# An attention and expert-layer kernel: one more PSUM bank for transposes, router steps in another order, part of v from another queue

## The chip, the core and the metric

The kernel runs on one core of a Trainium2 chip. The metric is the device time of one execution in microseconds (us). The engines are TensorE (PE: matmuls and transposes, with PEld for its weight loads), VectorE (DVE), ScalarE (ACT), GpSimd (POOL) and SyncE (SP). They run side by side and wait for each other through semaphores. Transfers from and to DRAM are issued by SP or GpSimd and carried out by 16 DMA engines. Matmul results land in PSUM, eight banks of 128 x 512 numbers, and from there ScalarE or VectorE copies them to SBUF.

## The reference

There are 8 batches, 8 heads, 576 positions of width 64. Attention works within chunks of 64 positions; its result is read as 4608 tokens of width 512. Each token goes to one of 16 experts (4 groups of 4).

```python
scores = scale * np.matmul(q_c, k_c.transpose(0, 1, 2, 4, 3))        # per chunk of 64
attn = np.exp(scores - scores.max(-1, keepdims=True))
attn = attn / (attn.sum(-1, keepdims=True) + 1e-09)
x = (attn @ v_c) ...                                                 # 4608 x 512
g_idx = np.argmax(x @ w_group, axis=1)                               # softmax weight g_w
for g in range(4):
    xg = x[g_idx == g]
    e_idx = np.argmax(xg @ w_expert[g], axis=1)                      # softmax weight e_w
    for e in range(4):
        h = np.maximum(xg[e_idx == e] @ w1[g, e], 0.0)               # 512 -> 1024
        out[tokens of g, e] = (g_w * e_w)[:, None] * (h @ w2[g, e])  # 1024 -> 512
```

## The kernel before

**Stages.** Up to about 200 us a loop walks over 36 token tiles of 128 tokens (two chunks). Until about 245 us a hand-written tail finishes attention and routing and begins the first expert. Then a loop over units runs the experts: a unit is up to 256 tokens of one expert, and GpSimd gathers its rows from the DRAM buffer `xs` and scatters its results to the output.

**A step of the token loop.** The order on TensorE, ScalarE and VectorE is the order of the source; SP's and GpSimd's streams are ordered by the scheduler. Step t is a row of short names (function `run`): `b` scores of tile t (L312), `s` maximum and subtraction on VectorE (m L320, pr L324), `p` attention times v of tile t-2 (L349), `n` its normalisation into x (L365), two `a` (transposes of q and k for later tiles, L293, copied out at L297), `c` transposes of the exponentials of tile t-1 (L337, copied at L339), `e` the exponential (L331), `x` transposes of x of tile t-3 (L377, copied at L378).

**The router.** Every four tiles, `1` multiplies the transposed x with the router weights (L384) and ScalarE copies the logits to `lts` (L386); `2` transposes them back (L394 to L397); `3` ranks the tokens by matmuls (L485, L486). Between these, VectorE works through `route` and `place`, generators of which the helper `more` runs a step at a time between its other instructions; Ls, mx, one, ls (L410 to L420) come first, then ScalarE's exponential `ex` (L426). At the end GpSimd scatters the tiles' rows to `xs` (L512).

**PSUM banks.** The transposes `a`, `c` and `x` take turns with three banks (pool `pst`, tile `tp`). The router's three products share one bank, `lgk`, through the helper `bank`; the tail gives them a bank of the pool instead. Scores and outputs have two banks each.

**Loads.** q and k come in 512-KB pieces (L256) and v per head and batch: 64 partitions x 9 chunks x 256 bytes (L274), into two buffers used by turns. All of them are issued by SP, in one queue. GpSimd issues the scatters of x, and the weights and rows of the first expert (L183, L187, L562).

**Experts.** Token numbers and gate weights of a unit stand in the last two columns of its gathered rows. GpSimd copies them to `in_`, and once the scatter of the unit before has landed, from `in_` to `io_`, which VectorE multiplies with (L1045, L1049) and the scatter takes its row numbers from (L1308).

## Time and profile before

| | us |
|---|---|
| three runs | 700.09, 707.25, 702.55 (median 702.55) |
| profiled execution | 695.77, its span 694.1 |
| TensorE busy | 613.5 (88% of the span) |
| VectorE busy | 396.6 (57%) |
| ScalarE busy | 325.5 (47%) |
| GpSimd busy | 154.9 (22%) |

The profile covers one execution. A row of its timeline gives start, duration, engine, line of the kernel, operation and tiles, and in brackets how long the engine had been idle and what ended that. The view of waits sums such idle times by the instruction that waited and the one that released it. PEclk is the granted TensorE clock as a share of full speed. The DMA column is the mean busy share of the 16 DMA engines; it can pass 1 where transfers of two queues overlap on an engine.

### The profile page before, as it was taken

The numbers are of one execution on the slowest core, as the hardware profiler recorded it, in microseconds if no ns is written. First come the engines' busy times: TensorE is split into PE (matmuls) and PEld (weight loads), VectorE is DVE, ScalarE is ACT, GpSimd is POOL, SyncE is SP. The second block draws the span as 40 slices with busy tenths as digits, with TensorE's granted clock in tenths as the row PEclk, the third lists the DMA queues.
The fourth block names the chain that finished last, engine by engine and source line by source line (L and its number), as shares of the span: only waits on it lengthen the run. The fifth ranks groups of instructions, "written<-read, shape, count | busy, mean of one in ns | idle before, by whom it ended". The sixth has DMA issues, their size and how long they took to land.

```text
span 694.1 us, 16755 instructions
## 1 busy us (share of the span) xinstructions
PE 613.5 (88%) x5866; PEld 537.3 (77%) x5867; DVE 396.6 (57%) x731; ACT 325.5 (47%) x450; POOL 154.9 (22%) x256
## 2 busy tenths in 40 slices
PE   5678777777698889999899999999999999999991
PEld 4567666656576778998888889898998998898980
DVE  2557777877657657721267875572622777853220
ACT  2567777876744244611237555151611574551110
POOL 0000222223533322122123331222212212322110
PEclk9988999997879989999999999999999999999996
DMA  9989999999831298841074985644341667831000
GB/s 188 219 168 249 247 185 228 219 265 224 252 123 62 92 343 306 288 138 62 26 289 152 332 310 185 222 171 170 155 155 60 236 233 255 324 121 56 30 30 15
DMA packets 116852, 128.13 MB, mean 185 GB/s; under 512 B 49406, under 2 KB 84478, under 8 KB 116800
## 3 DMA queue, kind: packets, MB, share of 16 engines
q1 hardware_dynamic: 105936, 93.76, 48.2%
q0 software_dynamic: 10864, 33.64, 14.3%
q8 instruction: 37, 0.61, 0.4%
q14 instruction: 15, 0.12, 0.1%
HBM read 106.23 MB, written 21.93 MB: 185 GB/s over the span
## 4 chain that ended last, share of the span: by engine, by line
PE 72%; DMA 6%; DVE 6%; ACT 5%; SPq 5%; issue 3%; DVEq 0%; POOL 0%; ACTq 0%; POOLq 0%
PE py L844 26%; PE ph L829 18%; PE lgk L829 6%; PE ph L813 5%; DMA va<-in_v_dram 5%; SPq L256 2%; ACT qT L297 2%; PE tp L293 2%; PE tp L377 2%; PE py L861 2%; PE pxt L729 2%; SPq L274 1%; PE o L349 1%; PE sc L312 1%; PE ph L775 1%
## 5 line engine op out<-in xcount | busy, mean ns | idle before, releaser
L829 PE MATMUL ph<-xt,w1h 128*128 128x256 f32 x672 | 102.1, 289 | 5.4 <-issue 5.4
L829 PEld LDWEIGHTS ph<-xt,w1h 128*128 128x128 f32 x672 | 92.4, 198 | 7.2 <-issue 6.2
L984 ACT ACTIVATE hth<-ph 128x512 fp32r<-128x512 f32 x43 | 25.7, 598 | 153.3 <-PE ph L829 151.0
L1308 POOL DMA_INDIRECT out_dram<-xl,io__3479 x37 | 39.1, 1056 | 157.1 <-DVE xl L1045 141.5
L1059 DVE TENSOR_TENSOR w2l<-w2r,w2h 128x1024 fp32r<-128x1024 f32 x60 | 69.5, 1221 | 7.5 <-ACT w2h L999 5.3
L1055 DVE TENSOR_TENSOR w1l<-w1r,w1h 128x2048 fp32r<-128x2048 f32 x28 | 63.2, 2292 | 13.7 <-ACT w1h L971 11.9
L844 PE MATMUL py<-w2h,hth 128*128 128x512 f32 x264 | 67.7, 398 | 0.0
L844 PE MATMUL py<-w2l,hth 128*128 128x512 f32 x264 | 65.3, 389 | 0.0
L844 PE MATMUL py<-w2h,htl 128*128 128x512 f32 x264 | 65.2, 389 | 0.0
L1045 DVE TENSOR_SCALAR xl<-py,io__3479 128x512 f32<-128x512 f32 x33 | 24.7, 750 | 67.7 <-PE py L844 67.3
L1078 DVE SCALAR_TENSOR_TENSOR htl<-ph,hth 128x512 fp32r<-128x512 f32 x40 | 27.4, 688 | 60.3 <-ACT hth L984 59.7
L844 PEld LDWEIGHTS py<-w2l,hth 128*128 128x128 f32 x264 | 49.6, 188 | 10.6
L844 PEld LDWEIGHTS py<-w2h,htl 128*128 128x128 f32 x264 | 49.6, 188 | 10.3
L829 PE MATMUL ph<-xt,w1l 128*128 128x256 f32 x336 | 55.5, 288 | 0.5 <-DVE w1l L1055 0.5
L293 PE MATMUL tp<-cs,qk 128*128 128x128 f32 x272 | 49.0, 311 | 7.6 <-DMA qk<-in_q_dram 5.8
L844 PEld LDWEIGHTS py<-w2h,hth 128*128 128x128 f32 x264 | 47.6, 188 | 10.2 <-ACT hth L1030 0.9
L971 ACT CAST w1h<-w1r 128x2048 fp32r<-128x2048 f32 x28 | 52.2, 1903 | 4.5 <-DMA w1r<-in_moe_w_dram 2.7
L297 ACT COPY qT<-tp 64x512 f32<-64x512 f32 x68 | 41.9, 616 | 23.6 <-PE tp L293 22.9
L975 ACT CAST w2h<-w2r 128x2048 fp32r<-128x2048 f32 x28 | 52.3, 1924 | 0.0
L512 POOL DMA_INDIRECT xs<-x,pos x24 | 23.7, 986 | 119.2 <-DMA va<-in_v_dram 69.9
L829 PEld LDWEIGHTS ph<-xt,w1l 128*128 128x128 f32 x336 | 47.7, 197 | 0.7 <-DVE w1l L1055 0.7
L293 PEld LDWEIGHTS tp<-cs,qk 128*128 128x128 f32 x272 | 35.1, 159 | 16.9 <-issue 13.2
(269 smaller groups left out, 1067.9 us busy)
## 6 DMA issues: line engine op xcount, KB each, us to landing
w1r<-in_moe_w_dram SPq DMA_DIRECT2D x30, 1024.0 KB, 6.2
w2r<-in_moe_w_dram SPq DMA_DIRECT2D x30, 1024.0 KB, 6.8
xgr<-xs POOLq DMA_DIRECT2D x38, 257.0 KB, 5.4
va<-in_v_dram SPq DMA_DIRECT2D x56, 144.0 KB, 6.4
qk<-in_q_dram SPq DMA_DIRECT2D x11, 512.0 KB, 6.1
qk<-in_k_dram SPq DMA_DIRECT2D x11, 512.0 KB, 7.1
w1r<-in_moe_w_dram POOLq DMA_DIRECT2D x2, 1024.0 KB, 10.0
w2r<-in_moe_w_dram POOLq DMA_DIRECT2D x2, 1024.0 KB, 7.6
```

The costliest lines, as they stand in the source:

```text
L293: nc.tensor.transpose(pt[:, hp, :], st["q", n // 4][:, z, 2 * hp + x], ident)
L297: (nc.vector.tensor_copy if z and not a else nc.scalar.copy)(to[:, a], pt[64 * a:64 * a + 64])
L813: m = pe.matmul(ph[n], a_[:, c, 0:P], w_[:, c, n * 512:(n + 1) * 512], start=(i == 0), stop=(i == 11))
L829: m = pe.matmul(ph[f // 2][:, f % 2 * 256:f % 2 * 256 + 256], w_[:, c, f * P:(f + 1) * P], a_[:, c, :], start=(i == 0), stop=(i == 11))
L844: m = pe.matmul(py[j], a_[:, f, half[j]], w_(b, f), start=(i == 0), stop=(i == 23))
L971: lambda b, s, j: ac.copy(wt[b][0][:, s], w1r[j]), K1)
L975: lambda b, s, j: ac.copy(wt[b][2 + j], w2r[j]), K2)
L984: ac.activation(hth()[:, 2 * b:2 * b + 2, :], ph[b].rearrange("p (f t) -> p f t", f=2), AF.Relu).then_inc(S["Ha"], 1)
L1055: lambda b, s, j: ve.tensor_sub(wt[b][1][:, s], w1r[j], wt[b][0][:, s].bitcast(F32)), K1, js)
L1059: m = ve.tensor_sub(wt[b][4 + 2 * j + i], w2r[j][:, 2 * i:2 * i + 2], wt[b][2 + j][:, 2 * i:2 * i + 2].bitcast(F32))
L1078: ve.scalar_tensor_tensor(out=htl()[:, 2 * b:2 * b + 2, :], in0=ph[b].rearrange("p (f t) -> p f t", f=2), scalar=0.0, in1=hth()[:, 2 * b:2 ...
L1308: gp.indirect_dma_start(out, bass.IndirectOffsetOnAxis(ap=io[:, j, 0:1].bitcast(I32), axis=0), yb[:, j, :], None, bounds_check=N - 1, oob_ ...
```

## The change

- `bank` now deals out four banks by turns in the token loop: every fourth request, of transposes and router products alike, gets `lgk`. In the tail (`turn[0] = -1`) it deals out the pool's three, and `lgk` is used where it was before.
- The `lts` copy is a step of its own (`l`) and stands behind the first `a`; in the tail `l7` and `l8` stand one and two names further on than the copies did. `3` moves to the end of its step. The first part of each router generator, which reads a bank, runs at once behind the maximum `m` of the next step (`read_banks`). `ex` is issued two router steps later.
- v of batches 1 to 4 is loaded by GpSimd.
- Unit numbers go to two buffers by turns; `in_` and the second copy are gone, and the unit's code on GpSimd and VectorE stands twice, chosen by the unit's number.

```diff
+                (nc.gpsimd if 0 < b < 5 else nc.sync).dma_start(vbufs[b % NV][64 * x:64 * x + 64, j:, hp, 0:HD],
                                   v[b, h, j * CH:, :].rearrange("(c s) d -> s c d", s=CH))
 
             def stage_a(n):
...
                     st["T", u, i] = kpool.tile([P, 4, 512], F32, name="kT" if i else "qT", tag="qkT")
                 dst = st["T", u, i % 2]
-                pt = ps_t.tile([P, 4, P], F32, name="tp")
+                pt = heads4(bank())
...
 
-            def bank(end):
-
-                return ps_t.tile([P, 4, P], F32, name="tp").rearrange("p a b -> p (a b)") if end else lgk
+
+            turn = [0]
+
+            def bank():
+                turn[0] += turn[0] >= 0
+                if turn[0] > 0 and turn[0] % 4 == 3:
+                    return lgk
+                return ps_t.tile([P, 4, P], F32, name="tp").rearrange("p a b -> p (a b)")
+
+            heads4 = lambda z: z.rearrange("p (a b) -> p a b", a=4)
...
@@ -318,6 +325,7 @@
                 sc = s["sc"]
                 m = rpool.tile([P, 2, 4], F32, name="m")
                 nc.vector.tensor_reduce(out=m, in_=sc, axis=AX.X, op=ALU.max)
+                read_banks()
                 more()
 
...
             def stage_e1(g):
                 xT = st["xT", g]
-                lt = bank(g >= GL - 1)
+                lt = bank()
                 for c in range(4):
                     nc.tensor.matmul(lt[32 * c:32 * c + 32, :], lhsT=wg[:, c, :], rhs=xT[:, c, :], start=True, stop=True)
+                st["lt", g] = lt
+
+            def stage_lts(g):
                 lts = xtpool.tile([P, 512], F32, name="lts")
-                nc.scalar.copy(lts, lt)
+                nc.scalar.copy(lts, st["lt", g])
                 st["lts", g] = lts
 
             def stage_e2(g):
                 lts = st["lts", g]
-                lg = lgk
+                lg = lgk if turn[0] < 0 else bank()
                 for i in range(NG):
...
                 st["lg", g] = lg
-                routing.append(route(g))
+                (first if turn[0] >= 0 else routing).append(route(g))
...
                 ex = rpool.tile([P, R5, 4], F32, name="ex")
-                nc.scalar.activation(ex, ls, AF.Exp)
+                if fast:
+                    nc.scalar.activation(ex, ls, AF.Exp)
                 yield
                 V.tensor_reduce(out=mx, in_=one, axis=AX.X, op=ALU.min)
                 yield
+                if not fast:
+                    nc.scalar.activation(ex, ls, AF.Exp)
                 V.tensor_tensor(out=one, in0=one, in1=mb, op=ALU.is_equal)
...
-                rk = bank(g >= GL - 2)
+                rk = bank()
...
-                    routing.append(take(cn, n))
-                routing.append(place(g))
+                    (first if turn[0] >= 0 else routing).append(take(cn, n))
+                (first if turn[0] >= 0 else routing).append(place(g))
                 if g == GC:
-                    routing.append(choose(cn))
+                    (first if turn[0] >= 0 else routing).append(choose(cn))
...
-            routing = []
+            routing, first = [], []
+
+            def read_banks():
+                while first:
+                    z = first.pop(0)
+                    if z.gi_code.co_name != "choose":
+                        next(z)
+                    routing.append(z)
...
                     if last(t - 4):
                         run("1%d" % ((t - 4) // NG))
                     run("a%d" % (2 * t + 6) if t else FIRST)
-                    if last(t - 7):
-                        run("3%d" % ((t - 7) // NG))
+                    if last(t - 4):
+                        run("l%d" % ((t - 4) // NG))
...
                     run(" ".join("V%d" % n for n in VS.get(t, ())))
                     if last(t - 4):
                         run("2%d" % ((t - 4) // NG))
+                    if last(t - 7):
+                        run("3%d" % ((t - 7) // NG))
                     run(EXTRA.get(t, ""))
+                turn[0] = -1
                 run(TAIL)
...
-        io_, in_ = (fpool.tile([P, 2, 2], F32, name=n) for n in ("io_", "in_"))
+
+        io_ = [fpool.tile([P, 2, 2], F32, name="io%d" % i) for i in range(2)]
...
+        def by_turns(eng, u, f):
+            with eng.If((u & 1) == 0):
+                f(io_[0], io_[1])
+            with eng.Else():
+                f(io_[1], io_[0])
...
+                    def YE(j, io):
+                        return ve.tensor_scalar(out=yb[:, j, :], in0=py[j], scalar1=io[:, j, 1:2], scalar2=None, op0=ALU.mult)
+
+                    def YEh(u, j, n, io):
+                        g, y = io[0:64, j, 1:2], yb[0:64, j, :]
...
+                        def out_(io, _):
+                            def free():
                                 W("Is", 2 * u)
                                 W("Sc", 32 * u)
-                                W("L2", 2 * u + 2)
-                                YEh(u, 0, 2)
+
+                            with ve.If(k > 1):
+                                free()
+                                W("L2", 2 * u + 1)
+                                YE(0, io).then_inc(S["Y"], 1)
...
+                        by_turns(ve, u, out_)
...
-                        W("Is", 2 * u)
-                        W("XT", 2 * u + 4)
-                        carry2(in_, xg[:, :, D:XW], "In")
-                        W("In", 2 * u)
-                        gather(ra[0], 0)
-
-                        with gp.If(ra[1] < mr):
-                            gather(ra[1], 1)
+                        def unit(io, nxt):
+                            W("XT", 2 * u + 4)
+                            W("Sc", 32 * u)
+                            carry2(nxt, xg[:, :, D:XW], "Is")
+                            W("Is", 2 * u + 2)
+                            gather(ra[0], 0)
+
+                            with gp.If(ra[1] < mr):
+                                gather(ra[1], 1)
+                            with gp.Else():
+                                gp.dma_start(xg[0:1, 1, 0:1], xs[mr:mr + 1, 0:1]).then_inc(S["Gb"], 16)
+                            scatter(2 * u + 2, 0, io)
+                            with gp.If(k > 1):
+                                scatter(2 * u + 2, 1, io)
+                            with gp.Else():
+                                gp.dma_start(word, xs[mr:mr + 1, 0:1]).then_inc(S["Sc"], 16)
+
+                        by_turns(gp, u, unit)
```

ScalarE's stream at the second router step of the loop, with the copies and exponentials of two token steps; before:

```order
L386 COPY lts<-lgk 128x512
L297 COPY qT<-tp 64x4x128 x2
L339 COPY pT<-tp 128x512
L331 ACTIVATE pr<-pr 128x512
L297 COPY kT<-tp 64x4x128
L378 COPY xT<-tp 128x4x128
L426 ACTIVATE ex<-ls 128x80
L297 COPY qT<-tp 64x4x128 x2
```

and with the change:

```order
L297 COPY qT<-lgk 64x4x128 x2
L397 COPY lts<-tp 128x512
L347 COPY pT<-tp 128x512
L339 ACTIVATE pr<-pr 128x512
L297 COPY kT<-tp 64x4x128
L386 COPY xT<-tp 128x4x128
L443 ACTIVATE ex<-ls 128x80
L297 COPY qT<-tp 64x4x128 x2
```

The lts copy has moved behind the two copies of qT; ex has kept its place, and some copies now read the bank `lgk`.

VectorE's stream at the head of the step that follows, where the router's numbers are first read; before:

```order
L320 TENSOR_REDUCE m<-sc 128x8
L410 TENSOR_REDUCE Ls<-lgk 128x80
L414 TENSOR_REDUCE mx<-Ls 128x20
L324 TENSOR_TENSOR pr<-sc,m 128x2x4x64
L418 TENSOR_TENSOR one<-Ls,mx 128x80
L420 TENSOR_TENSOR ls<-Ls,mx 128x80
L424 SCALAR_TENSOR_TENSOR one<-one,cs 128x80
```

and with the change:

```order
L327 TENSOR_REDUCE m<-sc 128x8
L421 TENSOR_REDUCE Ls<-tp 128x80
L425 TENSOR_REDUCE mx<-Ls 128x20
L429 TENSOR_TENSOR one<-Ls,mx 128x80
L431 TENSOR_TENSOR ls<-Ls,mx 128x80
L332 TENSOR_TENSOR pr<-sc,m 128x2x4x64
L435 SCALAR_TENSOR_TENSOR one<-one,cs 128x80
```

The two steps that end in ls now stand ahead of the subtraction pr.

GpSimd's stream from its first fills on (`va_131` and `va_129` are the two buffers of v, `xs` the scatter's target); before:

```order
L115 MEMSET pad 128x1
L603 CAST identr<-cs 128x128
L363 CAST x<-cs 128x4 x2
L363 CAST xl<-cs 128x4
L512 DMA xs<-x,pos 75904x514 x4
L363 CAST x<-cs 128x4
L512 DMA xs<-x,pos 75904x514 x4
```

and with the change:

```order
L371 CAST x<-cs 128x4
L371 CAST xl<-cs 128x4
L274 DMA va_129<-in_v_dram 64x9x64 x8
L274 DMA va_131<-in_v_dram 64x9x64 x4
L526 DMA xs<-x,pos 75904x514 x4
L274 DMA va_131<-in_v_dram 64x9x64 x4
L371 CAST x<-cs 128x4
L274 DMA va_129<-in_v_dram 64x9x64 x2
L526 DMA xs<-x,pos 75904x514 x4
L274 DMA va_129<-in_v_dram 64x9x64 x4
```

The 32 loads now stand among the scatters; the eight of batch 1 (`va_131`) come ahead of the rows shown, among the first fills.

## Rows read from the trace of the kernel before

**Rows 1.** Busy time of each engine in three stretches; the last columns as headed.

```profile
core 0: us, PE busy (x) PEld busy (x) DVE busy (x) ACT busy (x) POOL busy (x), PEclk, DMA share, GB/s
...
26.00:164.00 138.00, 107.37 (x2293) 87.44 (x2292) 100.41 (x299) 102.60 (x178) 21.90 (x26) 0.95 1.05 226
164.00:200.00 36.00, 26.94 (x410) 22.71 (x411) 23.70 (x60) 22.43 (x40) 19.86 (x21) 0.69 0.82 214
...
245.00:694.00 449.00, 427.83 (x2659) 384.44 (x2657) 235.80 (x258) 174.96 (x192) 96.75 (x181) 0.97 0.51 179
```

**Rows 2.** The same view, first and last of four groups of four token tiles.

```profile
58.00:77.80 19.80, 15.96 (x333) 13.09 (x332) 15.00 (x45) 14.67 (x27) 3.04 (x3) 0.91 1.09 247
...
116.30:135.40 19.10, 15.54 (x337) 12.31 (x336) 15.85 (x59) 15.14 (x28) 3.36 (x5) 1.00 1.08 226
```

**Rows 3.** Waits of ScalarE, 26 to 164 us: total us, times, longest.

```profile
ACT qT L297 <- PE tp L293: 12.3, 8, 5.9
ACT ex L426 <- DVE ls L420: 10.2, 6, 2.1
ACT lts L386 <- PE lgk L384: 8.7, 6, 1.9
```

**Rows 4.** Waits of TensorE in the same stretch.

```profile
PE tp L377 <- ACT qT L297: 16.4, 23, 2.1
PE o L349 <- DMA va<-in_v_dram: 8.7, 7, 3.7
```

**Rows 5.** Timeline of TensorE: start, duration, engine, line; idle time before it in brackets.

```profile
38.79 0.69 PE L312 MATMUL sc<-kT,qT 64*64 64x64 f32 x32
...
42.46 0.69 PE L312 MATMUL sc<-kT,qT 64*64 64x64 f32 x32
...
48.13 0.94 PE L349 MATMUL o<-va,pT 64*64 64x65 f32 x6 [3.66 <-DMA va<-in_v_dram]
...
52.61 0.70 PE L312 MATMUL sc<-kT,qT 64*64 64x64 f32 x15
```

**Rows 6.** Busy time and granted clock (PEclk) behind the stall.

```profile
48.00:54.00 6.00, 5.87 (x86) 5.22 (x86) 1.95 (x5) 3.55 (x6) 0.00 (x0) 0.54 1.07 258
```

**Rows 7.** Timeline of all engines around one router step.

```profile
94.97 0.59 ACT L386 COPY lts<-lgk 128x512 f32<-128x512 f32 x1 [1.19 <-PE lgk L384]
...
95.52 1.24 ACT L297 COPY qT<-tp 64x512 f32<-64x512 f32 x2
...
97.31 0.60 PE L397 MATMUL lgk<-cs,lts 128*128 128x128 f32 x4
...
99.98 0.68 DVE L324 TENSOR_TENSOR pr<-sc,m 128x512 f32<-128x512 f32 x1
...
100.57 0.23 DVE L418 TENSOR_TENSOR one<-Ls,mx 128x80 f32<-128x80 f32 x1
...
100.99 0.27 ACT L426 ACTIVATE ex<-ls 128x80 f32<-128x80 f32 x1 [1.81 <-DVE ls L420]
```

**Rows 8.** Issue of v on SP: ns least, median, most; first and last start.

```profile
L274 SPq DMA_DIRECT2D va<-in_v_dram x64: 595/976/4343, 12.7 to 170.2; - x64
```

**Rows 9.** Timeline of GpSimd: a weight load and a scatter that it issues.

```profile
170.82 0.78 POOL L187 DMA_DIRECT2D w2r<-in_moe_w_dram  x1
...
183.62 0.96 POOL L512 DMA_INDIRECT xs<-xl,pos  x1 [0.30 <-issue]
```

**Rows 10.** DMA packets from 4 to 8, 24 to 28 and 42 to 150 us.

```profile
DMA packets 3709, 0.93 MB, mean 233 GB/s; under 512 B 3709, under 2 KB 3709, under 8 KB 3709
...
DMA packets 2249, 1.13 MB, mean 283 GB/s; under 512 B 41, under 2 KB 2249, under 8 KB 2249
...
DMA packets 49475, 23.99 MB, mean 222 GB/s; under 512 B 24972, under 2 KB 47484, under 8 KB 49456
```

**Rows 11.** Waits of TensorE and VectorE, 245 to 694 us: total us, times, longest.

```profile
PE ph L829 <- issue: 5.4, 2, 3.5
...
DVE xl L1045 <- POOL io__3479 L1303: 0.4, 1, 0.4
```

## The prediction

> **What bounds the kernel now.** I read the stages first. After 245 us TensorE is busy 427.8 of 449 us, VectorE half of it and ScalarE less [rows 1]: the expert stage is TensorE's. Before 164 us no engine is full over the stretch: TensorE 107, VectorE 100, ScalarE 103 of 138 us, with the DMA engines' share at 1.05. A group of four token tiles there takes 19.8 us at the start and 19.1 us later, while ScalarE is busy 14.7 to 15.1 us of it and VectorE 15.0 to 15.9 [rows 2]. So 4 us per group are waits, and the list of waits says whose. On ScalarE, six waits of 8.7 us together stand before the copy of the router's logits (lts), six of 10.2 us before the router's exponential (ex), and 12.3 us before copies of transposed q, which are TensorE being late [rows 3]. TensorE is late for two reasons: 16.4 us for a PSUM bank that ScalarE has not emptied, and 8.7 us for v from DRAM [rows 4]. [...]

> **ScalarE's router steps and the fourth bank.** These go together, because neither pays alone. Per group, ScalarE loses 8.7/6 = 1.45 us at lts and 10.2/6 = 1.70 us at ex. The lts copy now stands behind the two q copies (1.24 us). TensorE's router matmuls are done by then, so I take that wait as gone. The ex instruction keeps its place between xT and qT on ScalarE, though the source issues it later: what moves is its input. On VectorE ls now comes before the subtraction pr, and pr took 0.59 us from its start to the next (99.98 to 100.57) [rows 7]. What remains: from the second router step on TensorE (97.31) to ex (100.99) were 3.68 us [rows 7]; without pr 3.1, with a hand-over of some 0.2 ahead of it 3.3 us after lts ends. ScalarE's own work between lts and ex was 3.62 us (from 95.56 to 99.18, where its wait of 1.81 begins) and loses the q copies, so 2.4 us. So 0.9 us of waiting stays, and I add 0.25 because kT on ScalarE follows kT on VectorE, which does the router steps of that tile first. Gain per group: 1.45 + 1.70 - 0.9 - 0.25 = 2.0 us. Without the fourth bank TensorE would not get ahead: its 16.4 us of bank waits put it in step with ScalarE, and lts would push the next transposes back. The extra bank removes these waits, but in plain steps it wins nothing itself, as ScalarE is busy nearly all of them. The router step runs seven times in the loop; five lie in the stretch that ScalarE and VectorE hold. The last two lie where v and the first weights arrive, and count 1 us together. Sum: -11 us. Bounds: 0, if another engine holds the pace, and 7 x 3.15 = -22 us.

> **v of batches 1 to 4 on GpSimd.** Taken off SP's queue are 32 loads at a median of 0.98 us [rows 8], 31 us of issue in which q and k stood behind v. What waited for these four batches on TensorE is 3.66 us and then 2.3 of the 8.7 us; the rest belongs to batch 5, which stays on SP. With the slow clock the first stall cost 10.15 - 3.67 = 6.5 us. Gain at most 6.5 + 2.3 = 8.8 us; I take 7. GpSimd issued no load of 256-byte runs before, so its price is bounded: a weight load of 512 runs took it 0.78 us, an indirect scatter of 128 rows 0.96 us [rows 9]; a v load has 64 x 9 = 576 runs, so 0.8 us or 4.5 x 0.96 = 4.3 us. The weight load is the same kind of instruction, so I take 0.8 us. The loads of batches 3 and 4 also stand between the scatters of x in that queue, 4 x 1.3 us each time; the step that needs them is five tiles (18 us) after the buffer is free. Scatters behind a load that waits for its buffer cost nothing until the first expert is chosen.

> Against it: batch 1 is now issued in the first 10 us, beside the q and k that everything waits for. Its 8 x 576 packets are 4608/927 = 5.0 us of the DMA engines at the highest rate seen (3709 packets in 4 us) [rows 10]. Some of it falls where SP's own issue is the limit; I charge +2 us, with ends 0 and +5.

> [...]

> **Do the DMA engines allow it?** From 42 to 150 us they moved 24972 packets under 512 B, 22512 under 2 KB and about 6.1 MB of larger ones [rows 10]. At the best rates of the other two rows (927 per us, 562 per us, 283 GB/s) that is 27 + 40 + 21 = 88 of 108 us. The terms above would take 17 us from this stretch and leave 91: room, but hardly any. I charge +3 us, with ends 0 and +10.

> **Unit numbers in two buffers.** GpSimd saves one pair of small copies per unit, and VectorE no longer waits for them: that wait appears once, for 0.4 us. TensorE's longest sum of waits in the stage is 5.4 us of issue, in two pieces, and none is put down to these copies [rows 11]. Its matmuls cover this part; 0 us. The row gather still waits for the scatter before it, as ahead of the change. Two copies of the unit's code on GpSimd and VectorE could cost a first fetch; at most the 3.5 us of the longest issue wait, so 0 to +3.5. The two moved lts copies in the tail, 0.59 us each, stand between work that waits for other things: 0, within 1 us either way.

> **Sum.** -11 - 7 + 2 + 3 + 0 = -13 us. The profiled execution took 695.77 us (span 694.1 and 1.7 around it), so 682.8; the median of the runs shown is 702.55, 6.8 above it. Forecast against that median: **690 us**. With the terms' ends near each other it would lie between 680 and 697.

> **Rivals.**
> - **DMA holds the pace.** The floor of 88 us is made of best rates over 4 us; if these cannot be held, the stretch shrinks little, and the late stretch (164 to 200 us, DMA share 0.82, TensorE at 0.69 of its clock [rows 1]) takes back what comes early. For it: a share near 1 throughout. Against it: SP was held by buffers and its own issue, and ScalarE's waits are tied to router steps, not to loads. The two stalls of batches 2 and 4 and a third of the ScalarE term remain: -2 - 4 + 3 = -3, about 699.5 us.
> - **All waits go.** Router -16 (seven at 2.3), v -8.8, nothing lost at the start: 25 us less, with some contention 22: about 680 us. Against it: VectorE, at up to 15.9 us per group, would have to be full.
> - **GpSimd is too slow for v (slower).** Eight loads and, for batches 3 and 4, one round of scatters (5.2 us) must pass the queue in an 18 us window, so it decides from (18 - 5.2)/8 = 1.6 us per load on. At the upper bound of 4.3 us the three batches are 16, 21 and 21 us late. Somewhat above midway between the ends, at 2.8 us, they are 4, 10 and 10 us late: 24 us, less 6.5 for the stall of batch 1 that still goes and two thirds of the router term (7), with 2 for the start: +12, about 714.5 us, which I take. For it: 256-byte runs from GpSimd have no row. Against it: the weight load's 0.78 us.

> [...]

> **How the numbers follow.** Forecast 0.53, DMA holds 0.21, all waits go 0.12, GpSimd too slow 0.14. About 1% (7 us) is what a measurement can tell from no change: faster is below 695.5, slower above 709.6. Faster: 0.53 x 0.93 + 0.12 + 0.02 = 0.63; slower: 0.09 (two thirds of the last rival, whose mild cases stay below 709.6) + 0.02 = 0.11; same 0.26. The range from 678 to 703 takes in the forecast, the first rival and most of the second, and leaves out about 0.2.

> **What would show it.** In the changed trace: ScalarE's wait before lts gone and that before ex near 0.9 us; a group of four tiles in 16.5 to 17.5 us; TensorE's waits for ScalarE's bank nearly gone; no slow-clock stretch near 48 us; a v load on GpSimd issued in about 0.8 us. The expert stage should keep its length within 2 us. It is wrong if groups keep 19 us, if TensorE waits for v of batches 2 to 4 for more than 3 us each, or if the expert stage moves.

## The result, and the profile after

Over twenty runs each the changed kernel took 705.4 us (698.96 to 711.12) against 699.28 (691.58 to 707.25): a ratio of **1.0102, 95% interval 1.0073 to 1.013**, so 6 to 7 us slower (the medians differ by 6.1) where 690 was forecast. A ratio leaves out every run over 1.5% above the fastest of its kernel; under the first heading of the experiments that drops 11 of the 27 runs of the kernel before and raises the ratios, so the medians of all runs stand beside them there. The profiled execution took 705.49 us, span 703.5.

The windows by stage answer to [rows 1] (columns as there):

```profile
26.00:164.00 138.00, 102.85 (x2159) 83.59 (x2160) 94.55 (x278) 96.05 (x167) 38.20 (x49) 0.93 0.99 212
164.00:200.00 36.00, 23.39 (x436) 19.36 (x434) 21.30 (x60) 24.71 (x45) 17.39 (x18) 0.88 1.08 237
255.00:703.00 448.00, 427.38 (x2673) 383.44 (x2671) 236.57 (x259) 176.11 (x194) 89.88 (x139) 0.98 0.51 180
```

In the same 138 us ScalarE did 167 pieces of work instead of 178: by 164 us fewer tile steps are done. The expert stage is not slower. From its first matmul (240.02 us, before 228.09) to the end it lasted 463.5 us, before 466.0. So the whole loss lies ahead of it, and the start of the tile steps on TensorE says where:

| start of, us | before | changed | difference |
|---|---|---|---|
| step 2 | 26.34 | 34.40 | +8.1 |
| step 7 | 52.61 | 52.37 | -0.2 |
| step 12 | 78.31 | 82.11 | +3.8 |
| step 18 | 106.82 | 109.25 | +2.4 |
| step 19 | 110.55 | 120.53 | +10.0 |
| step 27 | 150.36 | 157.79 | +7.4 |
| expert stage | 228.09 | 240.02 | +11.9 |
| end of the span | 694.1 | 703.5 | +9.4 |

The four groups from step 12 to step 28 took 19.1, 24.7, 19.4 and 21.2 us, before 19.5, 19.0, 19.1 and 21.0: none came near the 16.5 to 17.5 us forecast.

Waits of ScalarE from 26 to 164 us, total, times and longest, against [rows 3]:

```profile
ACT qT L297 <- PE tp L293: 15.6, 8, 5.4
ACT qT L297 <- PE lgk L293: 11.9, 5, 5.8
ACT ex L443 <- DVE ls L431: 7.3, 5, 2.2
ACT kT L297 <- DVE kT L297: 4.0, 5, 0.8
```

The wait for lts is gone, as forecast. The one before qT grew from 12.3 to 27.5 us (two rows, since q transposes now use the router's bank, lgk, too). Waits of TensorE in the same stretch, against [rows 4]:

```profile
PE o L357 <- issue: 9.3, 3, 5.1
PE tp L293 <- DMA qk<-in_q_dram: 5.6, 1, 5.6
...
PE o L357 <- DMA va<-in_v_dram: 1.6, 2, 1.1
```

The 16.4 us for ScalarE's bank are gone, those for v fell from 8.7 to 1.6. The 5.6 us for q are one wait, at 31 us: batch 1's v now moves beside the q and k that the first steps need. The largest of the other new waits is put down to "issue", 9.3 us ahead of the products with v: TensorE waited for nothing that the profile shows. In the kernel before that row read

```profile
PE o L349 <- issue: 1.5, 2, 1.1
```

The longest such pause is the jump between steps 18 and 19. Timeline of TensorE and GpSimd there:

```profile
110.36 1.47 POOL L274 DMA_DIRECT2D va<-in_v_dram  x2 [0.27 <-issue]
110.44 0.45 PE L357 MATMUL o<-va,pT 64*64 64x65 f32 x12 [0.49 <-ACT pT L347]
115.97 0.92 PE L357 MATMUL o<-va,pT 64*64 64x65 f32 x20 [5.08 <-issue]
116.82 1.11 PE L293 MATMUL lgk<-cs,qk 128*128 128x128 f32 x4
```

TensorE stops for 5.08 us after 12 of the 32 products with v of step 16's tile. That tile belongs to batch 3, whose loads were issued at 83.64 us and earlier; the two loads issued at 110.36 are batch 4's, first needed two steps later. So the profile shows no wait for v here. Behind the pause its transposes take 1.06 to 1.11 us instead of 0.60 to 0.66. The DMA queues from 111 to 116 us (packets, MB, share of the 16 engines):

```profile
q0 software_dynamic: 201, 0.47, 54.3%
q1 hardware_dynamic: 851, 0.43, 52.2%
q8 instruction: 1, 0.02, 1.7%
q14 instruction: 1, 0.01, 0.8%
```

q0 is GpSimd's queue: with the 32 loads (4.72 MB) it moves 38.36 MB in the whole execution, before 33.64, and SP's q1 89.04, before 93.76. Both instruction packets started between 113 and 114 us (113.24 and 113.34), 2.7 and 2.6 us before TensorE went on (115.97).

Last, the issue of v by engine (ns least, median, most):

```profile
L274 POOL DMA_DIRECT2D va<-in_v_dram x32: 733/757/974, 1.5 to 111.1; - x32
```

GpSimd issues a load in 0.76 us: the price taken, 0.8, was right, and the rival by a slow GpSimd falls. The stall of batch 1 and the slow clock behind it [rows 6] are gone as well; the window there, changed:

```profile
48.00:54.00 6.00, 5.67 (x154) 4.91 (x151) 5.44 (x13) 5.83 (x11) 3.71 (x6) 1.00 0.91 248
```

Steps 2 to 7 now take 18.0 us instead of 26.3. So the change lost 8.1 us ahead of step 2 and won 8.3 by step 7.

### The profile page after: what moved, and what is told of

Its sections match the earlier page's. It is cut to its first block, busy times and chain, and to the rows that moved or that the text cites. A ratio compares the mean times of both kernels' runs of the same rounds, so it can differ in the third digit from the quotient of the medians.

```text
span 703.5 us, 16825 instructions
## 1 busy us (share of the span) xinstructions
PE 609.9 (87%) x5866; PEld 533.2 (76%) x5867; DVE 393.8 (56%) x731; ACT 324.7 (46%) x450; POOL 172.2 (24%) x244
## 2 busy tenths in 40 slices
DMA packets 99956, 128.13 MB, mean 182 GB/s; under 512 B 30975, under 2 KB 66559, under 8 KB 99905
## 3 DMA queue, kind: packets, MB, share of 16 engines
q1 hardware_dynamic: 86992, 89.04, 44.7%
q0 software_dynamic: 12912, 38.36, 17.9%
## 4 chain that ended last, share of the span: by engine, by line
PE 68%; DMA 7%; DVE 6%; SPq 6%; ACT 5%; issue 5%; POOL 1%; DVEq 0%; POOLq 0%; ACTq 0%
PE py L877 26%; PE ph L862 16%; PE lgk L862 5%; PE ph L846 5%; DMA va<-in_v_dram 3%; SPq L256 3%; DMA w1r<-in_moe_w_dram 2%; ACT qT L297 2%; PE sc L319 2%; PE o L357 2%; PE tp L293 1%; PE pxt L762 1%; PE tp L385 1%; SPq L267 1%; SPq L274 1%
## 5 line engine op out<-in xcount | busy, mean ns | idle before, releaser
L862 PE MATMUL ph<-xt,w1h 128*128 128x256 f32 x672 | 100.0, 285 | 4.8 <-issue 4.8
L862 PEld LDWEIGHTS ph<-xt,w1h 128*128 128x128 f32 x672 | 90.4, 194 | 6.5 <-issue 5.6
L1345 POOL DMA_INDIRECT out_dram<-xl,io x37 | 41.6, 1125 | 165.6 <-DVE xl L1078 151.0
L1078 DVE TENSOR_SCALAR xl<-py,io 128x512 f32<-128x512 f32 x33 | 24.7, 748 | 66.5 <-PE py L877 66.4
L1008 ACT CAST w2h<-w2r 128x2048 fp32r<-128x2048 f32 x28 | 52.4, 1927 | 0.7 <-DMA w2r<-in_moe_w_dram 0.7
L357 PE MATMUL o<-va,pT 64*64 64x65 f32 x1088 | 27.7, 232 | 24.4 <-issue 9.3
L1339 POOL COPY io<-xgr 128x2 int32<-128x2 int32 x23 | 10.2, 442 | 157.9 <-PE pxt L762 130.7
L293 PE MATMUL tp<-cs,qk 128*128 128x128 f32 x200 | 35.2, 304 | 10.9 <-DMA qk<-in_q_dram 7.5
L357 PEld LDWEIGHTS o<-va,pT 64*64 64x64 f32 x1088 | 22.6, 143 | 28.7 <-issue 10.7
```

The source lines that it names most:

```text
L293: nc.tensor.transpose(pt[:, hp, :], st["q", n // 4][:, z, 2 * hp + x], ident)
L357: nc.tensor.matmul(o[cols, x, hp * W:hp * W + W], lhsT=pT[rows, hp, cols], rhs=v_at(2 * t + c)[rows, hp], start=True, stop=True)
L862: m = pe.matmul(ph[f // 2][:, f % 2 * 256:f % 2 * 256 + 256], w_[:, c, f * P:(f + 1) * P], a_[:, c, :], start=(i == 0), stop=(i == 11))
L1008: lambda b, s, j: ac.copy(wt[b][2 + j], w2r[j]), K2)
L1345: gp.indirect_dma_start(out, bass.IndirectOffsetOnAxis(ap=io[:, j, 0:1].bitcast(I32), axis=0), yb[:, j, :], None, bounds_check=N - 1, oob_ ...
```

## The experiments

Theories: **A**, the loads of v on GpSimd cost the time; **B**, full DMA engines set the pace and swallow what the engines win; **C**, the ring of banks and the later router steps cost it. Theories D to F are named where they are first expected. Runs that stand under one heading shared a chip. Ratios are against runs of the kernel before on that chip.

### One part at a time

`undo_v`: the change, with

```diff
-                (nc.gpsimd if 0 < b < 5 else nc.sync).dma_start(vbufs[b % NV]...
+                nc.sync.dma_start(vbufs[b % NV]...
```

> The change with the v loads of batches 1 to 4 back in SP's queue; ring of four banks, later router steps and two buffers of unit numbers stay. Theory A (the loads in GpSimd's queue cost the time: about 8 us at the start, where TensorE's tile step 2 began at 34.4 us instead of 26.3, and some more at the late loads of batches 3 and 4; the bank and router part gains): about 690 us against 699 before, ratio 0.987, tile step 2 near 26 us again and no stall of TensorE at step 18. Theory B (the DMA engines hold the pace, all that is won elsewhere is waited for at a transfer): 697 to 701, ratio 1.00, with TensorE's waits for v as long as before, 11 us. Theory C (the ring of four banks and the later router steps are themselves what costs): 704 to 707, ratio 1.01.

Measured: 1.0041 (1.0006 to 1.0077); medians 700.4 and 698.1 us. The 690 us of theory A did not come: without the loads on GpSimd, the other parts still gain nothing.

`v_alone`: the kernel before, with that line the other way round.

> The kernel before with one edit: v of batches 1 to 4 loaded from GpSimd's queue. Theory A: 706 to 714 us against 699, ratio 1.01 to 1.02, tile step 2 near 34 us and at least one wait of TensorE for v of over 4 us between 90 and 130 us. Theory B: 697 to 703, ratio 1.00, the same bytes come later or earlier but the last of them at the same time. Theory C: 692 to 697, ratio 0.99, as the prediction had it for this part (7 us less).

Measured: 1.0096 (1.005 to 1.0141); medians 701.8 and 698.1 us. One of its waits of TensorE from 26 to 164 us:

```profile
PE o L349 <- DMA va<-in_v_dram: 2.6, 2, 1.5
```

8.7 us of waiting for v became 2.6, and yet the kernel is slower. No wait for v of over 4 us came between 90 and 130 us, so theory A holds in the time and not in its reason. The profile shows where the time went: step 2 began at 34.90 us, step 7 at 56.76, the expert stage at 232.20, against 26.34, 52.61 and 228.09 in the kernel before. The 4.1 us by which the expert stage is late stand already at step 7, and in front of step 2 TensorE waited 4.6 us for q.

`b1_sync`: the change with `1 < b < 5`.

> The change, with v of batch 1 alone back in SP's queue; v of batches 2 to 4 stays with GpSimd. Theory A: the start is given back, tile step 2 near 26 us instead of 34.4, and what is left of the loss is the late loads: 696 to 700 us, ratio 0.995 to 1.00. If the 8 us at the start are made up later anyway, since step 7 began at 52.4 us in both kernels: 704 to 707, ratio 1.01, and the cost lies behind step 7. Theory B: 703 to 706. Theory C: 704 to 707.

Measured: 1.0107 (1.0065 to 1.015); medians 703.2 and 698.1 us. Step 2 began at 27.65 us, so the loads of batch 1 on GpSimd are what delayed it in the change. But step 7 began at 59.01: batch 2's loads left GpSimd at 42.73, ahead of the last of batch 1 on SP (45.93), and TensorE waited for batch 1:

```profile
52.87 0.48 PE L357 MATMUL o<-va,pT 64*64 64x65 f32 x4 [6.53 <-DMA va<-in_v_dram]
```

One loss was exchanged for another, so this run cannot say what batch 1 costs in the whole.

`ring_router`: the code ahead of the expert stage from undo_v, the expert stage from before.

> The kernel before with the ring of four banks and the later router steps alone: no load of v on GpSimd, unit numbers in one buffer. Theory A: 688 to 693 us, the same as with two buffers of unit numbers within 2 us, and the expert stage no shorter or longer than before by over 2 us. Theory B: 697 to 701. Theory C: 704 to 707. If it differs from the run with two buffers by over 3 us, the unit numbers are not free.

Measured: 1.0052 (1.0007 to 1.0097); medians 699.9 and 698.1 us. With undo_v beside it the two buffers of unit numbers are worth nothing either way, and the ring with the later steps gains nothing. Why, shows one group's last step (timeline of ScalarE and TensorE):

```profile
94.63 0.59 ACT L386 COPY xT<-lgk 128x512 f32<-128x512 f32 x1
...
95.27 1.07 PE L392 MATMUL tp<-xT,wg 128*32 128x512 f32 x8 [1.07 <-ACT xT L386]
96.27 0.65 PE L293 MATMUL tp<-cs,qk 128*128 128x128 f32 x4
96.96 1.25 ACT L297 COPY qT<-tp 64x512 f32<-64x512 f32 x2 [1.74 <-PE tp L293]
...
98.23 0.59 ACT L397 COPY lts<-tp 128x512 f32<-128x512 f32 x1
```

lts no longer waits, but the copy now ahead of it does: the q transposes (L293) stand on TensorE behind the router's eight matmuls (L392), which wait for xT from ScalarE. 1.19 us at lts [rows 7] became 1.74 us at qT. All of ScalarE's waits from 80 to 150 us sum to 14.2 us here and to 14.7 in the kernel before. The group takes 18.8 us (80.68 to 99.45), not 16.5 to 17.5.

### Light loads of v

In `before_light`, `ring_light` and `after_light` (the kernel before, ring_router and the change):

```diff
+                e = NCH if b < 3 else 1
-                ...dma_start(vbufs[b % NV][..., j:, hp, 0:HD], v[b, h, j * CH:, :]...
+                ...dma_start(vbufs[b % NV][..., j:e, hp, 0:HD], v[b, h, j * CH:e * CH, :]...
```

> The kernel before; the v loads of batches 3 to 7 are all issued, in their places, but each moves one of its nine chunks of 64 rows (16 KB instead of 144; the other chunks keep the v of an older batch). 5.2 MB of DMA traffic fall away, 24 us at the 215 GB/s that the first 200 us of the earlier runs show. Theory B (the DMA engines, 99% busy over the first 200 us, hold the pace of the tile steps): 675 to 686 us against 699, since the steps behind batch 3 (from about 85 us) then run as fast as TensorE, VectorE and ScalarE allow, a group of four tiles in 17 to 18.5 us instead of 19. If the engines and not the transfers hold the pace: 693 to 699, only some of the 11 us go in which TensorE waited for v.

> The kernel with the ring of four banks and the later router steps alone, with the same light v loads of batches 3 to 7. Theory B: the part then shows the gain that the transfers had hidden: 5 to 10 us less than the kernel before with light loads, about 668 to 680. If the part is worth nothing in itself (its waits only change places between the engines): within 3 us of the kernel before with light loads.

> The whole change with the same light v loads of batches 3 to 7. If the loss of the change over the ring alone comes from the transfers themselves (two queues that take each other's share of full DMA engines): within 3 us of the ring alone with light loads, apart from batch 1's v at the start, which keeps its full size. If it comes from GpSimd's order (loads of batches 3 and 4 queued behind its waits for scatters and for buffers): 5 to 10 us above the ring alone with light loads, with the stall of TensorE near step 18 still there.

Measured in all: 757.0, 736.7 and 738.3 us. These times cannot be compared, since other values of v send the tokens to other experts and the expert stage grows (which the expectations overlooked); the tile steps can be read. Two groups each of before_light and of ring_light:

```profile
78.69:97.31 18.62, 14.46 (x335) 11.66 (x335) 14.76 (x45) 15.04 (x27) 4.26 (x6) 1.00 0.69 184
97.31:117.98 20.67, 16.06 (x335) 13.04 (x334) 14.77 (x45) 15.04 (x27) 4.05 (x5) 0.92 0.64 153
```

```profile
80.62:99.40 18.78, 14.98 (x335) 11.94 (x334) 14.81 (x45) 14.48 (x26) 2.72 (x5) 1.00 0.60 166
99.40:118.43 19.03, 15.17 (x335) 12.11 (x334) 14.79 (x45) 14.88 (x27) 4.04 (x6) 1.00 0.65 173
```

The DMA share fell from 0.85 to 1.05 (the kernel before and ring_router, the same groups) to 0.60 to 0.69, and the groups are as long as ever. From step 12 to step 28 the transfers do not hold the pace: B falls there. Behind step 28 it stands. From there to step 35 the light kernels took 41.7, 42.4 and 41.5 us, the same three with full loads 45.5, 46.9 and 47.8; before_q_first below took 41.8 with full loads, so this is a sign and no proof. In after_light the pause at 111 us is 1.24 us.

So a share near 1 was no sign here that the transfers hold the pace, and two queues are not needed to pass 1. In the kernel before, from 108 to 109 us, SP's queue alone read

```profile
q1 hardware_dynamic: 560, 0.15, 121.6%
```

### The next wait, the start, and batch 4

`ring_q_first` and `before_q_first` (ring_router and the kernel before):

```diff
-                    if last(t - 4):
-                        run("1%d" % ((t - 4) // NG))
                     run("a%d" % (2 * t + 6) if t else FIRST)
+                    if last(t - 4):
+                        run("1%d" % ((t - 4) // NG))
```

> The kernel with the ring of four banks and the later router steps alone, and one exchange in the order: after a group's last tile the transposes of the next q stand on TensorE ahead of the router's eight first matmuls instead of behind them. Theory D (the wait for lts went, but ScalarE's next copy, qT, waits 1.7 us per group for q transposes that stand behind the same eight matmuls, so nothing was won): that wait goes too, the group of four tiles takes about 17.2 us instead of 18.8, and five to seven groups make 7 to 11 us: 689 to 693 us against 698, ratio 0.985 to 0.99. Theory B in what is left of it (full DMA engines set the pace once the engines want more): 696 to 700, with longer waits of TensorE for v or q.

> The kernel before with that exchange alone (q transposes ahead of the router's matmuls, the copy lts right behind qT by the same move; router's bank apart from the ring). Theory D: as much as with the ring, 689 to 694, since the eight matmuls in front of ScalarE's work are the cost and the banks are not; TensorE's waits for a bank stay, 15 to 21 us, and cost nothing. If the banks matter as the prediction had it: 4 us or more above the ring with the exchange.

Measured: 0.9977 (0.993 to 1.0023) and 1.0001 (0.9965 to 1.0038). In ring_q_first the waits at qT went, as theory D has it, but the gain did not come. ScalarE's waits from 80 to 150 us in ring_q_first:

```profile
ACT ex L443 <- DVE ls L431: 14.0, 3, 5.0
ACT ex L443 <- DVE one L429: 4.7, 1, 4.7
ACT kT L297 <- DVE kT L297: 3.3, 4, 0.9
```

Four waits before ex now cost 18.7 us; in ring_router, which had another chip, they were 5.0. The longest come from TensorE. Timeline of ring_q_first, with GpSimd's scatters:

```profile
96.13 0.98 POOL L526 DMA_INDIRECT xs<-x,pos  x1 [11.66 <-DVE rc L366]
97.42 0.96 POOL L526 DMA_INDIRECT xs<-x,pos  x1 [0.30 <-issue]
97.92 0.69 PE L319 MATMUL sc<-kT,qT 64*64 64x64 f32 x32
...
98.97 0.34 PE L357 MATMUL o<-va,pT 64*64 64x65 f32 x4 [0.26 <-issue]
...
100.40 0.35 PE L357 MATMUL o<-va,pT 64*64 64x65 f32 x5 [1.08 <-issue]
101.86 0.59 PE L357 MATMUL o<-va,pT 64*64 64x65 f32 x21 [1.11 <-issue]
102.04 0.69 DVE L327 TENSOR_REDUCE m<-sc 128x8 f32<-128x512 f32 x1 [4.21 <-remote]
...
103.86 0.27 ACT L443 ACTIVATE ex<-ls 128x80 f32<-128x80 f32 x1 [4.71 <-DVE ls L431]
```

While this group's scatters run, TensorE's matmuls come in bursts of four or five, with up to 1.11 us of idle time between them; VectorE goes on only when they end, after 4.21 us. So this chip does not show what the exchanged order is worth without the bursts.

`before_wg`: the kernel before, with

```diff
-w_group.rearrange("(c p) g -> p c g", p=P) ... s["x"][:, c * P:(c + 1) * P]
+w_group.rearrange("(p c) g -> p c g", p=P) ... s["x"][:, c:D:4]
```

and the same for w_expert.

> The kernel before with the router's weights loaded in 640 packets of 64 bytes instead of 2560 of 16 (a partition holds four rows next to each other, and the transposes of x take every fourth column). In the kernel before the DMA engines are busy at 5 to 22 GB/s for some 7 us around 44 to 52 us. Theory B for the start (up to about step 12 the transfers hold the pace): tile step 7 begins 3 to 5 us earlier, at 48 to 50 us, and the whole takes 2 to 5 us less, 694 to 696. If the engines hold the pace there too: 697 to 700, step 7 near 52.5.

Measured: 0.9957 (0.9874 to 1.004); medians 707.7 and 705.3 us. Step 7 began at 52.02 us, not at 48 to 50: the small packets do not hold the start.

`b4_sync`: the change with `0 < b < 4`.

> The change with v of batch 4 alone back in SP's queue; batches 1 to 3 stay with GpSimd. If the 5 us for which TensorE stood still inside the products with v at 111 us, with a pair of instruction packets moving at 113 us, come from the transfers of batch 4 that run in a second queue there: that pause falls under 2.5 us, step 19 begins at about 114 instead of 120.5, and the time is 699 to 702, ratio 1.00 to 1.005. If the pause has nothing to do with these loads: it stays at 5 us and the time at 704 to 707.

Measured: 1.0006 (0.997 to 1.0043). No pause of over 2.5 us; steps 18 and 19 began at 111.33 and 115.72.

### Gaps, and both remedies together

`before_again`: the kernel before, unchanged.

> The kernel before, unchanged, with a profile of its own beside the three that follow. In the four runs of the last group TensorE's matmuls came in bursts of one to five, 0.72 us apart, once per group of four tiles, with no wait on another engine (15 to 28 such gaps of over 0.2 us between 24 and 175 us, 8 to 13 us in all); the first profile of the kernel before has two, 1.5 us in all. If the gaps belong to the run and not to those kernels: over 8 us of them here too, and a group of four tiles in about 20.3 us. If they come from the exchanged order or the changed loads: under 2 us and 19.0 to 19.5 us.

A gap is here an idle time of TensorE of over 0.2 us that is put down to "issue". Measured: 701.9 us, and eleven gaps of 7.1 us in all. Timeline:

```profile
98.29 0.32 PE L349 MATMUL o<-va,pT 64*64 64x65 f32 x3
99.69 0.71 PE L349 MATMUL o<-va,pT 64*64 64x65 f32 x29 [1.08 <-issue]
99.94 0.69 DVE L320 TENSOR_REDUCE m<-sc 128x8 f32<-128x512 f32 x1 [2.50 <-PE sc L312]
...
102.23 0.27 ACT L426 ACTIVATE ex<-ls 128x80 f32<-128x80 f32 x1 [3.29 <-DVE ls L420]
```

All eight profiles under this heading and the one above have at least ten such gaps between 24 and 175 us, the others at most seven, whatever the kernel. ring_q_first has 18, of 13.4 us together. So they come with the chip or the execution and not with one kernel. On these two chips the kernel before itself took 705.3 and 703.0 us in the median, on the three of the other headings 698.1, 696.4 and 698.6. The ratios under these two headings therefore compare kernels that both have the bursts.

`ring_q_first_few`: ring_q_first with

```diff
-                for hp in range(4):
+                for hp in (0, 2):
-  o[cols, x, hp * W:hp * W + W], ... rhs=v_at(2 * t + c)[rows, hp]
+  o[cols, x, hp * W:hp * W + 2 * W], ... rhs=v_at(2 * t + c)[rows, hp:hp + 2]
```

> The ring with the exchanged order, and the products with v issued for two heads at a time: 8 instructions instead of 16 in each tile, each on 130 columns instead of 65, so the same columns pass through TensorE (for the second head of each pair the weights are those of the first, so its values are another product and the routing differs; only the tile steps are compared). Theory E (what holds TensorE in the gaps is the supply of its instructions): with a tenth to a fifth of its instructions gone the gaps fall under 3 us in all and the group takes 17.0 to 17.8 us. If the supply has nothing to do with it: gaps as in the other runs of this group, and 18.8 to 21 us.

Measured: 721.3 us (the routing differs), 16 products with v per tile instead of 32, fifteen gaps, 6.0 us in all; groups of 17.5, 21.0 and 20.8 us. The first group, with no gap in it, shows the order's own length; in the other two the gaps came in spite of fewer instructions, so theory E's under 3 us failed.

`ring_q_first_wg`: both edits together.

> The ring of four banks, later router steps, q transposes ahead of the router's matmuls, and the router's weights in 640 packets of 64 bytes: the parts that came out at or under 1.00. If they add: ratio 0.985 to 0.995. If what holds the steps is elsewhere (instructions, v): 0.995 to 1.003.

Measured: 1.0004 (0.997 to 1.0037). Nothing adds up, and no version beat the kernel before by more than the noise.

`b4_only`: the change with `b == 4`.

> The change with v of batch 4 alone on GpSimd's queue, batches 1 to 3 back with SP. If batch 4's loads are what cost (the change 1.010, with batch 4 on SP 1.001): ratio 1.008 to 1.015, and a pause of TensorE of over 3 us within the products with v between 105 and 122 us. If the cost is spread over the batches: 1.003 to 1.007.

Measured: 1.0026 (0.9992 to 1.0061), no pause of over 1.61 us. No loss of batch 4 alone is clear of the noise.

### The change and its parts side by side again

`late_scatter`: ring_q_first with

```diff
+                for i in range(8 if g < 7 else 0):
+                    nc.gpsimd.tensor_copy(slow, pos.unsqueeze(2).broadcast_to([P, NG, 128]))
```

> The ring with the exchanged order, and ahead of each of the first seven groups' four scatters eight copies on GpSimd that are of no use (5 to 8 us in all), so that the scatters leave that much later. In the runs of the last two groups TensorE's gaps without a wait lie between the first scatter of a group and 2 us after its last one, about 2 to 6 us behind the first one's issue. Theory F (GpSimd's transfers take TensorE's supply of instructions): the gaps move with the scatters, to 2 to 6 us behind the first one again, and lie in other matmuls of another tile step. If they belong to the place in the program (a fixed spot behind the router's transposes): they stay in the products with v of the first step of each group and lie ahead of the scatters.

Measured: 709.0 us. This profile has four gaps, only two of them behind step 12 (1.22 us at 110.8 and 3.52 us at 160.9), so what was to be moved hardly occurred: inconclusive. But a pause of 3.52 us with all of v on SP says that v on GpSimd is not needed for one. Its group without a gap took 17.6 us (80.74 to 98.37).

`after_again` and `undo_v_again`: the change and undo_v, unchanged.

> The change, unchanged, on one chip with the run that follows. If the loads on GpSimd carry the loss on every chip: 0.5 to 1 percent above the change with v on SP, and 1.005 to 1.012 against the kernel before. If the loss was that of one chip (with batch 4 alone taken away another chip gave 1.001): equal within 0.3 percent.

> The change with v of all batches on SP, unchanged, beside the whole change on the same chip. 1.000 to 1.006 against the kernel before; 0.5 to 1 percent under the whole change if the loads on GpSimd cost on this chip too.

Measured: 1.0055 (1.0018 to 1.0093) and 1.0002 (0.9964 to 1.0039), medians 703.1 and 698.46. Timeline of TensorE and GpSimd in after_again:

```profile
81.73 0.69 PE L319 MATMUL sc<-kT,qT 64*64 64x64 f32 x32
...
82.25 0.28 PE L357 MATMUL o<-va,pT 64*64 64x65 f32 x4
83.40 0.97 POOL L526 DMA_INDIRECT xs<-x,pos  x1 [0.30 <-issue]
84.36 3.06 POOL L274 DMA_DIRECT2D va<-in_v_dram  x4
85.63 1.13 PE L357 MATMUL o<-va,pT 64*64 64x65 f32 x28 [3.10 <-issue]
86.69 1.11 PE L293 MATMUL tp<-cs,qk 128*128 128x128 f32 x4
```

Step 12 began at 81.73 us here and at 81.09 with v on SP, step 13 at 90.30 and 84.38: one pause of 3.10 us and the slow matmuls behind it make 5.3 us of the 6.0 by which the expert stage began later (234.81 against 228.82).

## Why the prediction was wrong

**The step that failed first is "Gain per group: 1.45 + 1.70 - 0.9 - 0.25 = 2.0 us", the term of -11.** Measured for that part: ratios of 1.0002 to 1.0052, 0 to +3.6 us. The wait at lts went, but I had counted as gain a wait whose cause stayed: the eight matmuls behind xT delay ScalarE's next instruction instead. Before ex 1.25 us a time stayed in the loop (5.0 in four), not 0.9. That the bank waits win nothing in plain steps was right: 16.4 us of them vanished without a trace in the time. And even with the next wait taken away, groups of 17.5 us come out singly, and the time does not fall; since those runs met the bursts, what that order is worth without them stays open.

**The second is the price of batch 1 at the start, "I charge +2 us, with ends 0 and +5".** It measured 8.1 us (step 2 at 34.40 instead of 26.34), and 7.3 between after_again and undo_v_again (35.38 and 28.07). The gain beside it, "Gain at most 6.5 + 2.3 = 8.8 us; I take 7", came true between steps 2 and 7 (8.3 us), and so did what it rests on: 0.76 us per load, waits for v from 8.7 to 1.6 us, no wait for v near 48 us. Its 6.5 us are the step that waits (42.46 to 52.61) less the one before it (38.79 to 42.46) [rows 5]; the granted clock from 48 to 54 us, 0.54 before [rows 6], is 1.00 with the change. The two cancel, and at step 7 nothing is won (52.37 and 52.61 us). In v_alone the price was not made up: 4.1 us were left.

**The third was in no term: TensorE's pauses without a wait.** Of its gaps between 24 and 175 us, in the nine profiles with full loads that have no bursts:

| run | v of batches 1 to 4 from | gaps, us in all | expert stage begins, us |
|---|---|---|---|
| ring_router | SP | 1.1 | 229.33 |
| before | SP | 1.5 | 228.09 |
| undo_v_again | SP | 3.0 | 228.82 |
| v_alone | GpSimd | 4.5 | 232.20 |
| late_scatter | SP | 5.8 | 236.25 |
| undo_v | SP | 6.4 | 236.65 |
| after_again | GpSimd | 9.1 | 234.81 |
| b1_sync | GpSimd (2 to 4) | 9.3 | 239.72 |
| after | GpSimd | 12.7 | 240.02 |

From before to after the gaps grew by 11.2 us and the expert stage began 11.9 us later; from undo_v_again to after_again it was 6.1 and 6.0. So in these two pairs the gaps are as long as the whole delay. That v on GpSimd makes them is not shown. The longest, over 3 us, stand where GpSimd's queue takes 52 to 75% of the DMA engines, but one of 3.63 us (before_light) stands beside SP's queue alone, and undo_v and undo_v_again, one kernel, differ by 3.4 us.

That v on GpSimd costs time is shown twice: by v_alone (medians 3.7 us apart, ratio +1.0%) and by after_again beside undo_v_again (4.6 us apart on one chip). Its size is known to a few us only.

**DMA, +3, and its rival:** the forecast of 699.5 us came nearest, but its mechanism is refuted from step 12 to step 28 by the light loads. Behind step 28, near the late stretch that the rival names, the light kernels are 4 to 6 us shorter, so there it may hold; ahead of step 12 it stays open. **Unit numbers, 0:** no effect seen: the expert stage took 463.5 to 467.7 us in seven profiles with two buffers and 464.0 to 471.1 in nine with one, so the 2 us that it was to keep within are less than what it varies by. **GpSimd too slow:** nearest in direction to the result, wrong in mechanism.

The 31 us of issue taken from SP (32 loads at 0.98 us [rows 8]) bought nothing by themselves: v_alone, which changes only that, took 701.8 us against 698.1.

In the sum, 0 to +3.6 for the ring and +3.7 to +6.7 for v give +4 to +10, where 6 to 7 were measured. Open are how the loss is shared among batches 2, 3 and 4 (1.0006 without the last, 1.0026 with it alone, 1.0107 with all three, on three chips, two of them with bursts), and what makes the pauses longer in one execution than in another.

## What to carry to other kernels

Before counting a wait as gain, follow what the engine's next instruction needs: if it stands behind the same work on the same engine, the wait only changes its name, as here from 1.19 us at lts to 1.74 us at qT. A wait of an engine that is in step with a fuller one can be slack: 16.4 us of TensorE's waits for a bank went here, and the time did not fall. And moving loads to a second queue moved 31 us of issue here and no byte less (128.13 MB in the profiled execution of both kernels): price what then moves beside what the first steps wait for, and look at what else moves there, instruction packets too: each of the 45 gaps below ended 2.4 to 3.1 us after one of them had started.

## What was not expected of the hardware

TensorE stood still with no semaphore in sight, up to 5.08 us at a time. That it was waiting for its own instructions is an estimate from the packets beside these pauses; no wait in the profile says so. In the twelve profiles without bursts there are 45 gaps of over 0.2 us between 24 and 175 us. Every one of the 45 ends 2.4 to 3.1 us after a 16-KB packet of queue q8 has started. The twelve have 226 such packets in that stretch, one in 8 us, so by chance about one gap in eleven would. The pauses of over 3 us:

| run | pause, us | packet of q8 starts | TensorE goes on | q0 (GpSimd), q1 (SP), % of the DMA engines |
|---|---|---|---|---|
| after | 5.08 | 113.24 | 115.97 | 53.5, 53.0 |
| b1_sync | 5.05 | 115.23 | 118.03 | 51.7, 42.4 |
| before_light | 3.63 | 30.87 | 33.72 | 0, 122.5 |
| late_scatter | 3.52 | 158.39 | 160.88 | 72.2, 39.2 |
| after_again | 3.10 | 83.00 | 85.63 | 75.0, 26.7 |

Most of the 226 packets have no gap behind them. What sets the others apart is not shown.

The bursts are something else. In eight profiles of twenty, matmuls came in bursts some 0.7 us apart (weight loads of ring_q_first at 98.95, 99.70, 100.41, 101.15 and 101.86 us), many of them beside GpSimd's scatters, 6 to 13 us of gaps per execution. Most of those gaps keep no fixed distance to a packet of q8: from 77.5 to 158 us at least 7 of the 13 in ring_q_first and 8 of the 11 in before_q_first have none that started 2.4 to 3.1 us ahead of their end. What causes them is open.
